# Windowed attention on one core: PV of two pairs in every second session, whole-array projections in the sessions between

## The chip, the cores and the metric

The kernel runs on one core of a Trainium2 chip. The metric is the device time of an execution in microseconds (us). The time of an execution is some 1.7 to 2.1 us longer than the span that the profile shows for it, from the first to the last instruction.

## The reference

Two problems, A and B, with inputs of the same shapes, the outputs side by side. Each of them:

```python
B, S, D = 1, 2048, 1024
H = 32; Dh = D // H; W = 256
q, k, v = split((x @ wqkv).reshape(B, S, 3, H, Dh))        # cut
scores = einsum("bhqd,bhkd->bhqk", q, k) * Dh ** -0.5
mask = (i - j >= 0) & (i - j < W)                          # causal window of 256
p = softmax(where(mask, scores, -1e9))
return einsum("bhqk,bhkd->bhqd", p, v) @ wo                # all bfloat16
```

## The kernel before

The work is cut into 152 *sessions*. In each of them TensorE computes the scores of eight half-blocks (as 32x64 tiles) into four banks of PSUM, the memory that matmuls write to; these banks exist once (`st`). ScalarE takes one exponential of all of it (128x2048 elements, 1.88 us). GpSimd masks the edges of the window. VectorE adds two masked halves (`both`). Some sessions later comes *PV*: TensorE multiplies the probabilities of a *pair* of query blocks by V, and by ones for the softmax sums, as four 32-column tiles into an accumulator `acc`, of which there are two. VectorE then takes the norm of the pair: reciprocal, two shuffles, multiply. All that is left of TensorE's time is filled with *chains*: eight steps of a projection (Q/K, V or output) into one of two PSUM buffers `pp`, which a copy then empties.

A projection step has two forms, on the whole array or as four tiles of 32 columns. A change of tiling costs some 0.1 us, in which the array empties (the *drain*), so a session with PV takes the form that PV has:

```python
def by_columns(out, lo, hi, lhsT, rhs, start, stop):
    if whole[0]:
        nc.tensor.matmul(out[:, lo:hi], lhsT=lhsT, rhs=rhs, ...)
        return
    for c in range(0, P, 32):
        nc.tensor.matmul(out[c:c + 32, lo:hi], lhsT=lhsT[:, c:c + 32], rhs=rhs, ...,
                         tile_position=(0, c))
```

The copy goes to ScalarE or VectorE, whichever a clock model, run while the program is written, expects to be done first.

The loop, which decides the order on every engine:

```python
for now in range(END):
    forced(now)                                    # chains that are needed now
    whole[0] = not (due and due[0][0] <= now)      # no PV in this session
    session(now)                                   # scores, exponential, masks
    while due and due[0][0] <= now:
        _, pg, pk = due.pop(0)
        finish_norm(1)                             # all norms but the last
        pv(pg, pk)
    while edges_due and edges_due[0][0] <= now:
        edge(*edges_due.pop(0)[1:])                # the adds of a later PV
    emit(now, level(now) - fixed[now])             # projection steps
```

## Time and profile before

| | before |
|---|---|
| time, median of 3 runs | 618.74 us (618.34 to 621.06) |
| TensorE busy | 97%, 16665 matmuls |
| 16 KB packets of the instruction queue | 132 |
| exponential on ScalarE | 152 x 1878 ns |
| copy of a projection buffer | 584 ns on ScalarE; some 0.68 us on VectorE (42 of them) |
| reciprocal on VectorE | 128 x 953 ns |

TensorE bounds the kernel, so every lost microsecond is a halt of TensorE. The view of waits lists them by line and by what released them; the columns are us in all, times, and the longest. For the kernel before, its larger lines after the start:

```profile
PE acc L562 <- issue: 4.9, 10, 1.1
PE st L490 <- issue: 2.2, 3, 1.4
...
PE pp L199 <- issue: 0.9, 2, 0.5
...
PE pp L195 <- ACT vt L207: 0.3, 1, 0.3
```

Nearly all of it is put down to "issue": no semaphore is waited for. A buffer `pp` that isn't emptied in time shows only once, for 0.3 us. The same thing from the other side, the instructions that wait for the copies on ScalarE (line 207):

```profile
who waited for it (us, times):
  ACT pt L497: 12.8, 11
  ACT osb L207: 1.6, 2
  PEld pp L855: 0.4, 1
  PE pp L195: 0.3, 1
```

### The profile page before, as it was taken

How to read it: one execution, taken by the hardware profiler on the slowest of the kernel's cores; microseconds unless marked ns; L12 is line 12 of the kernel's file. 1: busy time of each engine (PE TensorE's matmuls, PEld its weight loads, DVE VectorE, ACT ScalarE, POOL GpSimd, SP SyncE). 2: the span in 40 equal slices, each digit the busy share in tenths (PEclk: the TensorE clock that was granted, in tenths of full speed). 3: DMA queues.
4: the chain of work that ended last, by engine and by line, in shares of the span. 5: the costliest groups of instructions: out<-in, count | busy, mean ns of one | idle time of the engine just before them, and what ended most of it. 6: DMA issues, size and time to landing. Idle time of an engine off the chain costs nothing.

```text
span 616.0 us, 36878 instructions
## 1 busy us (share of the span) xinstructions
PE 598.9 (97%) x16665; PEld 372.8 (61%) x16665; DVE 429.9 (70%) x1143; ACT 405.8 (66%) x372; POOL 372.1 (60%) x918
## 2 busy tenths in 40 slices
PE   8999999999999899999999999999999999999996
PEld 4666577657665666656565766756555765555443
DVE  1388878777877678776887757777878778788200
ACT  3667766877776668666676666667766767665332
POOL 0476767776766667675766667566666766665000
PEclk9999999999999999999999999999999999999999
DMA  9814110111024410346011010112021040114221
GB/s 234 176 47 133 37 39 5 39 37 39 5 46 76 95 38 4 67 104 123 29 38 39 4 39 4 39 37 64 29 53 40 5 106 12 56 55 131 70 78 64
DMA packets 86836, 36.00 MB, mean 58 GB/s; under 512 B 65552, under 2 KB 86160, under 8 KB 86672
## 3 DMA queue, kind: packets, MB, share of 16 engines
q1 hardware_dynamic: 85632, 33.31, 22.4%
q8 instruction: 132, 2.16, 1.5%
q10 hardware_dynamic: 1040, 0.26, 0.2%
q14 instruction: 32, 0.26, 0.2%
HBM read 17.83 MB, written 8.39 MB: 43 GB/s over the span
## 4 chain that ended last, share of the span: by engine, by line
PE 90%; issue 3%; POOL 2%; DMA 2%; DVE 1%; ACT 1%; SPq 0%; POOLq 0%; ACTq 0%
PE pp L199 46%; PE pp L195 22%; PE acc L562 13%; PE st L490 9%; DMA xT<-in_A_x_dram 2%; POOL diag L507 1%; POOL pt L518 1%; DVE both L529 0%; DVE rinv L575 0%; ACT pt L497 0%; SPq L603 0%; DVE wide L580 0%; ACT osb L207 0%; DVE top L585 0%; ACT vt L207 0%
## 5 line engine op out<-in xcount | busy, mean ns | idle before, releaser
L497 ACT ACTIVATE pt<-st 128x2048 bf16<-128x2048 f32 x152 | 285.5, 1878 | 90.2 <-PE st L490 63.1
L507 POOL TENSOR_SCALAR_AFFINE_SELECT diag<-pt 128x256 bf16<-128x256 bf16 x512 | 216.3, 448 | 194.3 <-ACT pt L497 180.5
L199 PE MATMUL pp<-xT,wqk 128*32 128x512 bf16 x3092 | 185.9, 379 | 0.4 <-issue 0.4
L575 DVE RECIPROCAL rinv<-acc 128x128 f32<-128x128 f32 x128 | 121.9, 953 | 62.1 <-PE acc L562 61.4
L518 POOL TENSOR_SCALAR_AFFINE_SELECT pt<-pt 128x512 bf16<-128x512 bf16 (+1 forms) x256 | 161.0, 647 | 0.0
L529 DVE TENSOR_TENSOR both<-diag,pt 128x512 bf16<-128x512 bf16 (+1 forms) x256 | 144.8, 602 | 15.1 <-POOL diag L507 11.1
L199 PEld LDWEIGHTS <-wqk 128*32 128x32 bf16 x3092 | 83.1, 97 | 63.3 <-issue 2.0
L199 PE MATMUL pp<-wv,xT 128*32 128x256 bf16 x2840 | 88.4, 273 | 0.5 <-issue 0.5
L199 PEld LDWEIGHTS <-xT 128*32 128x32 bf16 x2840 | 75.5, 97 | 6.6 <-issue 1.1
L490 PEld LDWEIGHTS <-kT 32*64 32x64 bf16 x3904 | 41.1, 103 | 57.6 <-issue 57.4
L490 PE MATMUL st<-qT,kT 32*64 32x64 bf16 (+4 forms) x3904 | 66.3, 236 | 2.3 <-issue 2.2
L580 DVE STREAM_SHUFFLE wide<-rinv 128x128 f32<-128x128 f32 x256 | 64.5, 297 | 0.0
L207 ACT CAST osb<-pp 128x512 bf16<-128x512 f32 (+1 forms) x58 | 33.5, 578 | 46.6 <-PE pp L195 29.3
L195 PE MATMUL pp<-xT,wqk 128*128 128x512 bf16 (+1 forms) x267 | 58.8, 367 | 1.1 <-DMA xT<-in_A_x_dram 1.1
L195 PE MATMUL pp<-wo_sb,oT 128*128 128x512 bf16 (+1 forms) x269 | 58.2, 373 | 0.4 <-ACT vt L207 0.3
L199 PE MATMUL pp<-wo_sb,oT 128*32 128x512 bf16 x1004 | 58.5, 379 | 0.0
L582 DVE TENSOR_TENSOR oT<-acc,wide 128x256 bf16<-128x256 f32 x128 | 54.4, 425 | 4.4
L562 PE MATMUL acc<-pt,vt 128*32 128x128 bf16 (+2 forms) x1792 | 50.8, 224 | 1.5 <-issue 1.4
L562 PEld LDWEIGHTS <-vt 128*32 128x32 bf16 x2816 | 42.4, 96 | 15.8 <-issue 5.2
L207 ACT CAST vt<-pp 128x512 bf16<-128x512 f32 x53 | 30.9, 584 | 20.4 <-PE pp L199 14.1
L207 ACT CAST qT<-pp 128x512 bf16<-128x512 f32 x51 | 29.8, 585 | 21.5 <-PE pp L199 13.8
L195 PEld LDWEIGHTS <-oT 128*128 128x128 bf16 x269 | 25.8, 98 | 29.8 <-issue 0.8
(47 smaller groups left out, 397.3 us busy)
## 6 DMA issues: line engine op xcount, KB each, us to landing
out_dram<-osb SPq DMA_DIRECT2D x63, 128.0 KB, 1.8
wqk<-in_B_wqkv_dram SPq DMA_DIRECT2D x32, 128.0 KB, 3.0
wqk<-in_A_wqkv_dram SPq DMA_DIRECT2D x24, 128.0 KB, 3.5
wo_sb<-in_A_wo_dram SPq DMA_DIRECT2D x16, 128.0 KB, 2.9
wv<-in_B_wqkv_dram SPq DMA_DIRECT2D x16, 128.0 KB, 2.9
wo_sb<-in_B_wo_dram SPq DMA_DIRECT2D x16, 128.0 KB, 2.6
oT<-in_A_x_dram SPq DMA_DIRECT2D x4, 256.0 KB, 5.0
wv<-in_A_wqkv_dram SPq DMA_DIRECT2D x2, 512.0 KB, 4.5
```

Source lines behind the costliest of these rows:

```text
L195: nc.tensor.matmul(out[:, lo:hi], lhsT=lhsT, rhs=rhs, start=start, stop=stop, skip_group_check=True)
L199: nc.tensor.matmul(out[c:c + 32, lo:hi], lhsT=lhsT[:, c:c + 32], rhs=rhs, start=start, stop=stop, tile_position=(0, c), skip_group_check=True)
L207: nc.scalar.copy(out=out, in_=in_)
L490: nc.tensor.matmul(scores[c * HALF:(c + 1) * HALF, r, a * HALF:(a + w_) * HALF], lhsT=kT[rows, keys], rhs=qT[rows, q:q + w_ * HALF], start ...
L497: nc.scalar.activation(out=pt[:, :, :n * HALF], in_=scores[:, :, :n * HALF], func=ACT.Exp, bias=-SHIFT, scale=cfg.scale)
L507: nc.gpsimd.affine_select(out=diags[(g, p)][:, :, h, lo:lo + HALF], in_=pt[:, :, a * HALF:(a + 1) * HALF], pattern=[[0, 4], [1, HALF]], co ...
L518: nc.gpsimd.affine_select(out=blk, in_=blk, pattern=[[0, 4], [-1, w_ * HALF]], compare_op=ALU.is_gt, fill=0.0, base=-HALF * (us[a][2] - 3) ...
L529: nc.vector.tensor_tensor(out=both[:, :, h, o:o + w_], in0=dg[:, :, h, o:o + w_], in1=pts[t][:, :, a:a + w_], op=ALU.add)
L562: nc.tensor.matmul(acc[32 * r:32 * r + 32, o:o + w_], lhsT=lhsT, rhs=src[:, r, :], start=(x == 0), stop=(x == len(moves) - 1), tile_positi ...
L575: nc.vector.reciprocal(out=inverses[0][:, turn % 2, :], in_=acc[:, 2 * P:3 * P])
L580: nc.vector.stream_shuffle(out=wide[:, h * P:(h + 1) * P], in_=inverses[0][:, turn % 2, :], mask=[16 * h] * 32)
L582: nc.vector.tensor_tensor(out=oTs[(pi, k)][:, t, (p % 2) * 256:(p % 2 + 1) * 256], in0=acc[:, 0:256], in1=wide[:], op=ALU.mult)
```

## The change

The intent: PV of two pairs is gathered in every second session (`PV_EVERY`), so that the sessions between have no PV and can run their projections on the whole array. That saves six of eight instructions a step. One more buffer each for the probabilities and the diagonal, and one x tile less to pay for them. The norms are finished ahead of a session with PV, and the adds stand ahead of it too.

```diff
-PT_BUFS = 5
-DG_BUFS = 4
+PT_BUFS = 6
+DG_BUFS = 5
+X_AHEAD = 1
+PV_EVERY = 2
@@
-    xpool = ctx.enter_context(tc.tile_pool(name="xT", bufs=NQ + 2))
+    xpool = ctx.enter_context(tc.tile_pool(name="xT", bufs=NQ + X_AHEAD))
@@
+    def edge_time(g, p):
+        return max(when(g, *e) for e in entries if e[1] // 2 == p) + PV_LAG - 1
+
     def pv_time(g, p):
-        return max(when(g, *e) for e in entries if e[1] // 2 == p) + PV_LAG
+        return -(-(edge_time(g, p) + 1) // PV_EVERY) * PV_EVERY
@@ def x_time(pi, k):
-        if k < 2:
+        if k < X_AHEAD:
             return begin(pi * T - 3) + 2 * k
-        return first_use(pi * T - 1, k - 2, 0) + 1
+        return first_use(pi * T - 1, k - X_AHEAD, 0)
@@
-    edges_due = [(d - 1, g, p) for d, g, p in due if p]
+    edges_due = [(edge_time(g, p), g, p) for _, g, p in due if p]
@@ in the loop, after the PV of this session
             finish_norm(1)
             pv(pg, pk)
+        if due and due[0][0] == now + 1:
+            finish_norm()
         while edges_due and edges_due[0][0] <= now:
             edge(*edges_due.pop(0)[1:])
```

## The prediction

> **What bounds the kernel now.** I read the page first: busy shares, granted clock, the chain that ended last.
>
> ```profile
> PE 598.9 (97%) x16665; PEld 372.8 (61%) x16665; DVE 429.9 (70%) x1143; ACT 405.8 (66%) x372; POOL 372.1 (60%) x918
> PEclk9999999999999999999999999999999999999999
> q8 instruction: 132, 2.16, 1.5%
> PE 90%; issue 3%; POOL 2%; DMA 2%; DVE 1%; ACT 1%; SPq 0%; POOLq 0%; ACTq 0%
> ```
>
> TensorE is busy 97% at full clock and carries 90% of the chain, so only its own stream and its pauses can move the end. Then the timeline of TensorE over two neighbouring sessions, the first without PV (projections on the whole array, 128*128), the second with PV (projections as four 32-column tiles, 128*32):
>
> ```profile
> 407.81 0.42 PE L490 MATMUL st<-qT,kT 32*64 32x192 bf16 x20
> 408.17 3.41 PE L195 MATMUL pp<-xT,wqk 128*128 128x512 bf16 x15
> 411.51 0.43 PE L490 MATMUL st<-qT,kT 32*64 32x64 bf16 x28
> 411.87 0.41 PE L562 MATMUL acc<-pt,vt 128*32 128x128 bf16 x12
> ...
> 412.44 1.47 PE L199 MATMUL pp<-xT,wqk 128*32 128x512 bf16 x24
> 413.73 1.48 PE L199 MATMUL pp<-wv,xT 128*32 128x256 bf16 x48
> ```
>
> The reader is to take start-to-start distances, because the durations overlap. 24 column matmuls are 6 groups of four: 413.73 - 412.44 = 1.29 us, 215 ns a group. 15 whole matmuls and the drain before the next scores: 411.51 - 408.17 = 3.34 us, or 15 x 216 ns and 0.1. So a 512-wide projection step costs 216 ns in both forms, and I find 109 against 109 ns for the 256-wide ones by the same reading. Each kind of session has about 0.50 us that is not streaming of PV or projections: 3.70 - 15 x 0.2133 for the first, 3.63 - 0.53 - 6 x 0.2133 - 12 x 0.1067 for the second.
>
> Last, what stops the stream: the timeline where a session takes 4.68 us rather than 3.6, and the DMA view of its start (211.9 to 213.1).
>
> ```profile
> 212.41 0.47 PE L490 MATMUL st<-qT,kT 32*64 32x64 bf16 x36
> 212.81 0.41 PE L562 MATMUL acc<-pt,vt 128*32 128x64 bf16 x20
> 213.05 0.28 PE L562 MATMUL acc<-diag,vt 128*32 128x128 bf16 x6
> 214.41 0.23 PE L562 MATMUL acc<-diag,vt 128*32 128x128 bf16 x2 [1.08 <-issue]
> ```
>
> ```profile
> q8 instruction: 1, 0.02, 5.0%
> ```
>
> TensorE halts after six of eight equal matmuls, in the middle of a group of four, where no semaphore is waited for. The idle time is put down to issue. In that stretch one packet of queue 8, the instruction queue, starts (at 212.03 by the trace's DMA records). I put the whole trace against the program order. Sixteen gaps between starts exceed 0.4 us in the same way. Their first matmul stands each time at place 194 or 195 modulo 256 of TensorE's program, and each comes 2.17 to 3.15 us after a packet of queue 8 began. Together they cost 11.2 us. Two packets of queue 8 never start less than 3.23 us apart. So these are waits for the next block of 256 instructions, and they come where instructions are short: scores, PV and 32-column V projections.
>
> **What the Trainium skill says.** "Runtime: NRT & Kernel Launch", section "Instruction fetch mechanics": the sequencer refills its memory in 16 KiB blocks of 256 instructions over its own DMA queue. The trace agrees: 132 packets, 2.16 MB, 16 KB each, and a halt only at block boundaries. The page also calls the cost of a crossing "mostly hidden"; 11.2 us are not hidden here. "TensorEngine Tiling (Array Packing)", section "Key Properties": a change of tiling mode drains the array. The trace agrees, with 96 to 107 ns beyond the stream ahead of each scores block. Its section "Restrictions" says that column tiling disables fast weight load, which would make whole-array projections cheaper. The trace shows no gain: loads of 97 to 98 ns in both forms, and 216 ns a step in both.
>
> **The change, part by part.**
>
> 1. *Whole-array projections in every second session.* From the program listings of the two kernels: groups of four column matmuls go from 1734 (773 Q/K, 710 V, 251 output) to 992 (402, 437, 153); whole ones go from 802 to 1544. Matmul work is the same. 742 steps convert at 0 ns each by the distances above, so the stream gains nothing. Each saves three loads and three matmuls: 742 x 6 = 4452 instructions of 33,330, 13%, or 17 of 130 blocks.
>
> 2. *PV of two pairs in one session.* The same 128 pairs, the same matmuls. Sessions with PV go from 119 of 152 to 75. A session has two mode changes either way (scores to PV and columns, or scores to whole, and back), and 0.50 us fixed in both kinds. Adding the read distances over both instruction lists, from the first scores to the last projection, gives 576.8 us before and 576.2 after: **-0.6 us**.
>
> 3. *The block waits.* Fewer instructions, but bunched: a double session has 256 to 368 (for instance 32 scores, 84 PV and 60 column matmuls, two instructions each, 352), one without PV 66 to 114 (before: 176 to 360 with PV, most of them under 280). I take for each block boundary the summed distances of the 288 instructions ahead of it (a block and the 32 by which I take the sequencer to lead) and compare this with a refill of 3.6 us, an estimate from packets of 3.2 to 4.4 us apart around the halts. Before: 20 of 128 blocks are shorter, by 5.4 us. After: 15 of 111, by 7.5 us; the worst takes only 2.1 us, the worst before 2.9. At 3.8 us it is 10.6 against 10.9. If a late refill also delays the next, it is 9.1 against 7.5 us at 3.6, and 17.5 against 10.9 at 3.8. This places most of the sixteen halts correctly, which is why I trust its form, though single halts come out too small. Fewer crossings in danger, each worse. I choose **-2.5 us** of the 11.2.
>
> 4. *Norms and adds ahead.* VectorE per pair: 0.953 for the reciprocal, 2 x 0.252 of shuffle, 0.425 for the multiply, half of 0.52, and 1.13 of adds: 3.27 us. Before, no TensorE halt of over 0.4 us falls on an accumulator or an add, so there is no wait to remove. After, two pairs bring 6.5 us of VectorE work into two sessions. In the first half these last 2 x 3.2 us by my sum, in the second 2 x 3.6. In the listing both norms stand ahead of the adds for the next pairs, so a late norm delays the adds, which end the next PV. At most three double sessions follow each other before a single one, so the debt stays below a microsecond: **+1.3 us**, perhaps 0.3 us in one of three double sessions of the first half.
>
> 5. *One x tile less, PT and diagonal buffers one more each.* Loads of the second problem's x come later and closer, 24 pieces of 3.6 us from issue to landing, and one session near the boundary grows to 6.6 us by my count while its neighbours shrink. The work is moved, not added: 0.
>
> Sum: -0.6 - 2.5 + 1.3 = -1.8 us. 618.7 - 1.8 = **617 us**.
>
> **The rivals.**
>
> *Fetch waits vanish.* If thinner sessions let the fetch run far enough ahead, all 11.2 us go: 618.7 - 0.6 - 11.2 = 607 us. For it: 13% fewer instructions, and a sparse session ahead of every dense one. Against it: the halts show one block of lead at most, and a double session can pass a whole block in 2.1 us.
>
> *Fetch waits get worse.* If most of the 48 sessions with 72 or more PV matmuls paid 0.3 us more than I take, it would be some 10 us: about 627 us. For it: blocks as short as 2.1 us, never seen before. Against it: the position of the boundaries varies, so most double sessions start with a fetched block in hand.
>
> *VectorE takes over.* With 6.5 us and a copy of 0.67 us in a 6.4 us double session, TensorE would wait for `both` or for an accumulator. Half a microsecond in each of some 25 double sessions of the first half would be +12 us, some 9 if the single ones between pay part of it back: about 625 us. Against it: VectorE is at 70%, and the listing gives it fewer copies than before.
>
> *Whole-array weight loads are faster after all.* At 5 ns a step, 742 steps would be 3.7 us: 613 us. The distances speak against it.
>
> **Range and chances.** The rivals reach 607 and 627, and neither is likely in full. The range is **610 to 623.5 us**. Faster by over 2% is below 606.4, which needs every fetch wait gone and no new wait: **4%**. Slower by over 2% is above 631, which needs a new regular wait: **5%**. Within 2%: **91%**.
>
> **What would show each step right or wrong.** Step 1: about 402 + 437 + 153 groups on the column line, at 216 and 109 ns from start to start. Step 2: the same fixed 0.50 us in both kinds of session. Step 3: 113 to 116 packets on queue 8, halts put down to issue and still ending 2.2 to 3.2 us after one, at fewer places, now in or just after the PV of double sessions. Step 4: TensorE waits of 0.2 to 0.6 us ahead of the last PV matmuls, ended by the adds, before 300 us and not after. Step 5: no TensorE wait on x between 190 and 300 us. I am wrong if the fetch waits fall below 4 us or rise above 15, if VectorE waits pass 5 us, or if a session without PV turns out to be bound by the exponential instead.

## More of the kernel before

The instructions of an engine stand in its program in the order in which they were emitted:

```python
def evacuate(out, in_, engines=("act", "dve")):
    if clock.evacuate(engines) == "act":
        nc.scalar.copy(out=out, in_=in_)
    else:
        nc.vector.tensor_copy(out=out, in_=in_)
```

## The result, and the profile after

| | before | after |
|---|---|---|
| time, median | 618.81 us (4 runs) | 623.56 us (623.12 to 624.22, 4 runs) |
| ratio | | 1.007 [1.0044, 1.0097] |
| span of the profiled execution | 616.0 us | 622.5 us |

Within 2%, but slower, where 1.8 us faster was predicted. The median lies at the upper edge of the predicted range, 0.06 us beyond it. Both kernels were run once more beside each other later: 615.78 us for before, 623.23 us for after, ratio 1.0125 [1.0102, 1.0147]. The loss is real.

The page of the changed kernel: busy times and counts, the instruction queue, and the chain that ended last.

```profile
PE 591.0 (95%) x14363; PEld 362.2 (58%) x14439; DVE 394.8 (63%) x1126; ACT 411.1 (66%) x389; POOL 360.6 (58%) x918
...
q8 instruction: 115, 1.88, 1.3%
...
PE 31%; POOL 4%; issue 3%; ACT 2%; DVE 0%; POOLq 0%; ACTq 0%
```

Three readings. There are 76 fewer matmuls than weight loads: records missing from this trace (the repeat has all 14439), so "PE 95%" is a little low and some lines of issue below are only holes in the record. ScalarE has 17 instructions more than before, VectorE 17 fewer: copies of projection buffers have moved from VectorE to ScalarE. And the shares of the chain add up to only some 40%, because it could not be followed back further; it isn't used.

The view of waits of TensorE in the changed kernel, same columns as above:

```profile
PE pp L197 <- issue: 7.7, 47, 0.4
PE pp L201 <- issue: 3.3, 6, 0.9
PE pp L197 <- ACT vt L209: 2.7, 6, 0.6
PE pp L197 <- ACT qT L209: 2.2, 5, 0.5
PE pp L197 <- ACT kT L209: 1.7, 5, 0.5
...
PE pp L197 <- ACT osb L209: 0.7, 2, 0.5
PE pp L197 <- POOL xT L382: 0.6, 1, 0.6
PE acc L567 <- DVE both L534: 0.3, 1, 0.3
```

The first line is mostly missing records (it is absent in the repeat). What is new are the four lines "<- ACT ... L209": a whole-array projection waits until a copy on ScalarE has emptied its buffer. From the side of the copies, in the same trace:

```profile
who waited for it (us, times):
  ACT pt L502: 29.3, 26
  PE pp L197: 7.4, 18
  ACT osb L209: 4.5, 6
```

TensorE waits for them 18 times where it was once, and always on the line of whole-array projections.

The views name only part of each halt, so I summed them from the trace itself: distances from the start of one matmul to the start of the next beyond what the first one streams, those over 0.12 us, after the first 16.2 us. A halt is called *block* where it comes at the place, modulo 256 instructions of TensorE's program, at which the prediction found its sixteen, and 2.1 to 3.6 us after a packet of the instruction queue began; the others are sorted by the two matmuls they lie between. Halts between two projection matmuls are called *buffer* (a copy is what releases nearly all of those for which the view names a releaser; one of 0.73 us in the changed kernel waits for an x tile instead), halts inside PV *PV* (an accumulator or the adds). The traces of before and both repeats are complete; sums from traces that lack records are less sure.

| us of halts (number) | block | buffer | PV | other | packets | span |
|---|---|---|---|---|---|---|
| before | 11.96 (24) | 1.05 (4) | 0.12 (1) | 0 | 132 | 616.0 |
| after | 6.57 (12) | 14.00 (31) | 0.48 (1) | 0.18 | 115 | 622.5 |
| before, repeated | 12.49 (23) | 1.02 (3) | 0.37 (1) | 0 | 132 | 616.2 |
| after, repeated | 5.19 (10) | 14.63 (32) | 0.48 (1) | 0.18 | 115 | 621.4 |

The spans differ by 6.5 us: -5.4 of block waits, +12.95 of buffers, +0.4 in PV, +0.2 elsewhere, which leaves -1.6 for everything else. In the repeat the same sum is -7.3 + 13.6 + 0.1 + 0.2, and -1.4 is left of the 5.2 us. So the change did take away about half of the block waits, and paid about twice as much (12.95 for 5.4 us, 13.6 for 7.3) with a wait that the kernel before hardly had.

What such a wait looks like: the timeline of a session without PV in the changed kernel (start, duration, engine, line, operation, count, and in brackets the idle time before it with what ended it).

```profile
123.18 0.42 PE L495 MATMUL st<-qT,kT 32*64 32x256 bf16 x20
...
123.73 1.88 ACT L502 ACTIVATE pt<-st 128x2048 bf16<-128x2048 f32 x1 [1.48 <-PE st L495]
123.76 1.89 PE L197 MATMUL pp<-xT,wqk 128*128 128x512 bf16 x8 [0.16 <-issue]
...
124.27 0.94 DVE L580 RECIPROCAL rinv<-acc 128x128 f32<-128x128 f32 x1
...
125.50 0.58 ACT L209 CAST qT<-pp 128x512 bf16<-128x512 f32 x1
125.79 0.42 DVE L587 TENSOR_TENSOR oT<-acc,wide 128x256 bf16<-128x256 f32 x1
125.97 0.60 ACT L209 CAST kT<-pp 128x512 bf16<-128x512 f32 x1
...
126.13 1.02 PE L197 MATMUL pp<-xT,wqk 128*128 128x512 bf16 x4 [0.48 <-ACT qT L209]
```

The same place in the repeat, whose trace lacks no matmul:

```profile
123.29 2.12 PE L197 MATMUL pp<-xT,wqk 128*128 128x512 bf16 x9
125.89 1.02 PE L197 MATMUL pp<-xT,wqk 128*128 128x512 bf16 x4 [0.48 <-ACT qT L209]
```

Before the scores, TensorE had all but the last step of a Q chain. The first step after the scores (the record that is missing in the first trace; the repeat has nine matmuls in place of eight) ends it, and from then on its buffer can be emptied. But ScalarE has just begun the exponential of 1.88 us, and VectorE is taking the norms of two pairs until after 126. So the copy waits until 125.5. TensorE meanwhile has eight steps for the other buffer, 8 x 0.216 = 1.73 us, fewer than exponential and copy together (1.88 + 0.58 = 2.46 us), and stands until the copy is done. In a session with PV, the PV matmuls lie between the scores and the projections, and take up much of that difference (0.57 us for one pair, from 411.87 to 412.44 in the timeline of the prediction).

### The profile page after: what moved, and what is told of

It reads as the page before. It is cut to its first block, busy times and chain, and to the rows that moved or that the text cites. A ratio compares the mean times of both kernels' runs of the same rounds, so it can differ in the third digit from the quotient of the medians. Undisturbed runs are those within 1.5% of the kernel's fastest.

```text
span 622.5 us, 32360 instructions
## 1 busy us (share of the span) xinstructions
PE 591.0 (95%) x14363; PEld 362.2 (58%) x14439; DVE 394.8 (63%) x1126; ACT 411.1 (66%) x389; POOL 360.6 (58%) x918
## 3 DMA queue, kind: packets, MB, share of 16 engines
q8 instruction: 115, 1.88, 1.3%
## 5 line engine op out<-in xcount | busy, mean ns | idle before, releaser
L534 DVE TENSOR_TENSOR both<-diag,pt 128x512 bf16<-128x512 bf16 (+1 forms) x256 | 117.4, 499 | 69.4 <-PE acc L567 52.2
L197 PE MATMUL pp<-xT,wqk 128*128 128x512 bf16 (+1 forms) x580 | 138.6, 373 | 13.4 <-issue 5.6
L197 PEld LDWEIGHTS <-wqk 128*128 128x128 bf16 x638 | 58.9, 98 | 72.6 <-issue 11.0
L201 PE MATMUL pp<-xT,wqk 128*32 128x512 bf16 x1608 | 97.4, 379 | 0.3 <-issue 0.2
L197 PE MATMUL pp<-wo_sb,oT 128*128 128x512 bf16 (+1 forms) x349 | 78.1, 374 | 3.2 <-issue 1.6
L197 PE MATMUL pp<-wv,xT 128*128 128x256 bf16 x587 | 71.6, 273 | 3.1 <-ACT kT L209 1.5
L209 ACT CAST osb<-pp 128x512 bf16<-128x512 f32 (+1 forms) x63 | 36.4, 579 | 43.3 <-PE pp L197 28.4
L197 PEld LDWEIGHTS <-xT 128*128 128x128 bf16 x587 | 55.5, 98 | 15.8 <-issue 4.6
L201 PEld LDWEIGHTS <-wqk 128*32 128x32 bf16 x1608 | 41.8, 97 | 32.5 <-issue 1.2
L201 PE MATMUL pp<-wv,xT 128*32 128x256 bf16 x1748 | 55.6, 273 | 3.1 <-issue 3.1
L201 PEld LDWEIGHTS <-xT 128*32 128x32 bf16 x1748 | 46.0, 97 | 8.6 <-issue 4.7
```

The lines of the kernel that those rows point to most:

```text
L197: nc.tensor.matmul(out[:, lo:hi], lhsT=lhsT, rhs=rhs, start=start, stop=stop, skip_group_check=True)
L534: nc.vector.tensor_tensor(out=both[:, :, h, o:o + w_], in0=dg[:, :, h, o:o + w_], in1=pts[t][:, :, a:a + w_], op=ALU.add)
```

## The experiments

The theory (T): the loss is the copy of a projection buffer that stands in ScalarE's order behind the exponential, in a session without PV, while VectorE, which could take it, is held by the norms that were put ahead. Rivals: (R1) VectorE's bunched norms and adds alone, which would show as waits in PV; (R2) instruction blocks, now needed faster in the double sessions; (R3) the whole-array form itself; (R4) the one x tile less. There were twelve runs, in three groups, the last group for repeats; each group has its own runs of the kernel before on its own chip (medians 618.84, 615.88 and 615.78 us), so I compare by ratio. All results were correct.

### The changed kernel without the norms put ahead

```diff
-        if due and due[0][0] == now + 1:
-            finish_norm()
```

> The changed kernel without the call that puts all norms ahead of the adds and copies in the session before a PV session; everything else kept. Theory (TensorE now waits for projection buffers in sessions without PV, because the exponential holds ScalarE and the bunched norms hold VectorE): VectorE gets free for copies earlier, so the buffer waits fall from about 12.8 us to 5 to 9 us and the time is 616 to 621 us. Rival (late adds and norms hold up PV, so putting them ahead helps): waits of PV for accumulators appear and the time is 626 us or more. If neither placement matters: 622 to 625 us.

Measured: 619.13 us, ratio 1.0006 [0.9976, 1.0035]. Buffer halts 4.94 us (from 14.00), block halts 4.97, but PV halts 8.26 us in 12 places (from 0.48). With VectorE no longer busy at this place, it takes 34 of the copies from ScalarE (355 instructions there, from 389), and most of the buffer waits go. What comes instead was no part of the theory, which therefore got its time (616 to 621 us) with one wait traded for another; the rival had named waits for accumulators. The timeline between the two PVs of a double session in this kernel:

```profile
122.25 0.28 PE L567 MATMUL acc<-both,ones 128*32 128x128 bf16 x8
...
123.06 0.42 DVE L587 TENSOR_TENSOR oT<-acc,wide 128x256 bf16<-128x256 f32 x1
...
123.53 0.41 PE L567 MATMUL acc<-pt,vt 128*32 128x64 bf16 x20 [1.00 <-DVE oT L587]
```

and its line in the view of waits:

```profile
PE acc L567 <- DVE oT L587: 6.1, 9, 1.1
```

The second PV needs the accumulator of the pair before, whose norm is only now being taken. So the two added lines do a job: two pairs in one session use up both accumulators, and both norms must be done before. They are needed, and they cost some 9 us of buffer waits where they stand.

### The changed kernel with PV in every session again

```diff
-PV_EVERY = 2
+PV_EVERY = 1
```

> The changed kernel with PV in every session again (pairs not bunched), with the one x tile less, the extra buffers and the norms put ahead kept. Theory: PV lies between the scores and the projections again, so the first projection chain ends after the exponential does and buffer waits fall under 4 us; halts for instruction blocks return to about 12 us; time 617 to 622 us. If the x tile or the norms' place cause the loss, the time stays at 623 to 626 us.

Measured: 628.73 us, ratio 1.0173 [1.0138, 1.0207]: a miss, slower than the changed kernel, whose ratio was 1.007 and 1.0125. Buffer halts fell to 2.14 us, as T has it (sessions without PV become few), and block halts are 7.97 us with 132 packets. But PV halts are 10.53 us in 29 places. In the view of waits, and in the timeline of one session:

```profile
PE acc L567 <- DVE both L534: 5.3, 15, 0.5
```

```profile
100.85 1.39 DVE L534 TENSOR_TENSOR both<-diag,pt 128x512 bf16<-128x512 bf16 x2
...
101.52 0.24 PE L567 MATMUL acc<-both,ones 128*32 128x128 bf16 x4
102.29 0.24 PE L567 MATMUL acc<-both,ones 128*32 128x128 bf16 x4 [0.53 <-DVE both L534]
```

PV now comes in nearly every session, so "the next session has PV" holds nearly always, the norm of the pair just accumulated is finished at once, and the adds stand behind it. That is R1, in the place in which the prediction had looked for it, but it takes this kernel to show it: the changed kernel has one such halt. The lines that put norms ahead belong to a plan with gaps between PVs.

### The changed kernel with projections in columns everywhere

```diff
-        whole[0] = not (due and due[0][0] <= now)
+        whole[0] = now < 4
```

> The changed kernel with all projections of the main loop as four 32-column matmuls. Theory (the whole-array form only saves instructions, hence instruction blocks): the buffer waits in sessions without PV stay at 10 to 13 us, the packets on queue 8 rise from 115 to about 148, the halts at block boundaries rise from 7 to 12 to 25 us; time 628 to 640 us. Rival (the whole-array form is faster by the step or by its drains): the same rise without more halts. If instruction blocks don't matter: 622 to 625 us.

Measured: 645.06 us, ratio 1.042 [1.0386, 1.0455], more than expected. Its instruction queue and its waits:

```profile
q8 instruction: 145, 2.38, 1.6%
```

```profile
PE pp L201 <- issue: 9.0, 13, 1.4
PE st L495 <- issue: 6.7, 12, 1.1
...
PE pp L201 <- ACT vt L209: 2.9, 7, 0.6
PE pp L201 <- ACT qT L209: 2.5, 6, 0.5
```

Buffer halts are 12.4 us (28), as in the changed kernel: they do not depend on the form of the projection, so R3 falls as their cause. Block halts are 25.25 us in 37 places, with 145 packets. That is R2 working the other way: more instructions for the same multiplications make more of these waits. Of the 21.8 us between the two spans (644.3 and 622.5 us), block halts make 18.7 and buffer halts -1.6; the other 4.7 us are not accounted for, so it is not shown that the column form costs nothing else.

### The changed kernel with an open chain finished ahead of the scores

In a session without PV, the chain that has begun is completed before the scores, so its copy is emitted before the exponential:

```diff
         forced(now)
+        if current and not (due and due[0][0] <= now):
+            emit(now, sum(ns for ns, _ in current))
         whole[0] = not (due and due[0][0] <= now)
         session(now)
```

> The changed kernel, but ahead of the scores of a session without PV the projection chain already begun is finished, so that its copy stands on ScalarE ahead of the exponential. Theory: one of the two buffers is free when the exponential starts, the buffer waits fall from about 12.8 us to under 4 us, and the time is 611 to 616 us, below both kernels. Rival (the waits come from elsewhere, or the later exponential holds up the next scores): 622 us or more.

Measured: 614.99 us, ratio 0.9939 [0.9908, 0.997]. Buffer halts 0.14 us, from 14.00, and the norms still stand ahead: T, by the direct edit. The copies are divided as in the changed kernel (386 instructions on ScalarE and 1129 on VectorE, where that has 389 and 1126), so it is their place that counts. The edit has one side effect: the steps moved ahead keep the form of the session before, often columns, so there are 420 matmuls more and 118 packets. The timeline of the same stretch of the program in this kernel:

```profile
126.31 0.42 PE L495 MATMUL st<-qT,kT 32*64 32x256 bf16 x20
126.43 0.58 ACT L209 CAST qT<-pp 128x512 bf16<-128x512 f32 x1 [1.14 <-PE pp L201]
126.66 2.76 PE L197 MATMUL pp<-xT,wqk 128*128 128x512 bf16 x11
...
126.91 1.88 ACT L502 ACTIVATE pt<-st 128x2048 bf16<-128x2048 f32 x1
```

The copy runs while TensorE does the scores, and the exponential follows it. TensorE goes on without a break. The price is a later exponential, which now sometimes holds the scores of the next session (PSUM banks `st`):

```profile
PE st L495 <- ACT pt L502: 2.6, 5, 0.8
```

That and PV halts of 1.23 us are far less than what was saved.

### Norms put off to the end of the session, in both versions

```diff
-        if due and due[0][0] == now + 1:
-            finish_norm()
         while edges_due and edges_due[0][0] <= now:
             edge(*edges_due.pop(0)[1:])
         emit(now, level(now) - fixed[now])
+        if due and due[0][0] == now + 1:
+            finish_norm()
```

On the changed kernel:

> The changed kernel with the bunched norms issued at the end of the session before a PV session, after its projections and their copies, in place of at its start. Theory (norms ahead of the copies hold the projection buffers; norms that are not done hold the second pair's accumulator): buffer waits near the 4.7 us of the kernel without the call, waits of the second pair for its accumulator well under the 8.3 us there, 1 to 4 us; time 613 to 618 us. If only the missing of PV ahead of the projections matters, buffer waits stay at 10 us or more and the time at 621 to 624 us.

and on the version with the chain finished first:

> Both mends together: the begun chain is finished ahead of the scores of a session without PV, and the norms are issued at the end of that session. Theory: buffer waits stay at about 0, the accumulator waits are 1 to 4 us, so no better than finishing the chain alone: 614 to 618 us. If the two add up: 610 to 613 us.

Measured: 620.23 us, ratio 1.0067 [1.005, 1.0084], and 621.67 us, ratio 1.01 [1.0068, 1.0131]. Both times are misses. The first has buffer halts of 4.74 us, as expected, but PV halts of 8.11 us, the same as with the two lines removed; the second has PV halts of 6.86 us and 1.81 us more between scores and PV. I had thought that the norms only had to be done at some time before the next PV. At the end of the session is too late: the accumulator is still held when the second PV begins. In the view of waits, first the one, then the other:

```profile
PE acc L567 <- DVE oT L587: 6.1, 9, 1.1
```

```profile
PE acc L567 <- DVE oT L587: 7.4, 10, 1.3
```

So the norms have to stand early, and the copy has to be kept out of their way. This is what the chain finished first does.

### The kernel before with whole-array projections in every session

```diff
-        whole[0] = not (due and due[0][0] <= now)
+        whole[0] = True
```

> The kernel before with all projections on the whole array, also right after a PV in the same session. Theory: a session with PV then has one more mode change, 0.10 to 0.13 us each in 119 sessions, 12 to 15 us in all, and the packets on queue 8 fall from 132 to about 92, with the halts at block boundaries falling from 12.0 us to under 3 us; time 617 to 626 us. If the halts are not due to blocks of instructions, they stay at 10 to 12 us and the time is 630 us or more. If whole-array steps are faster in themselves, it is under 614 us.

Measured: 615.46 us, ratio 0.9992 [0.9975, 1.0009], a little faster than expected. Its instruction queue:

```profile
q8 instruction: 92, 1.51, 1.0%
```

That is 92 packets, and **no** block halt at all, from 11.96 us. So R2's waits go entirely when the instructions become few enough. It gains nothing, because each session with PV now has one change of tiling more. The two neighbouring lines of its timeline:

```profile
411.08 0.28 PE L562 MATMUL acc<-both,ones 128*32 128x128 bf16 x8
411.29 0.94 PE L195 MATMUL pp<-wv,xT 128*128 128x256 bf16 x7
```

The median distance from the start of the last PV matmul to the first whole-array one is 151 ns, where the kernel before has 45 ns to the first column matmul: 106 ns more. (This trace lacks 123 matmuls, and both ends are recorded in 48 sessions only; a complete trace of the last version below has 152 ns.) The drain before the next scores, counted from the start of the last step's first matmul, is 96 ns in place of 107. That is 95 ns in each of some 118 sessions, 11.2 us, against 12 us of block waits saved.

### The kernel before with one x tile less

`X_AHEAD = 1` with its buffer count and its load times, and nothing else of the change.

> The kernel before with one x tile less alone, its loads placed as in the changed kernel. Theory: the tile has no part in the result, 617 to 621 us with about 12 us of block halts. Rival (later, closer loads of x hold up work near the change of problem): 622 us or more, with new waits between 190 and 310 us.

Measured: 618.98 us (617.05 to 619.98), ratio 1.0056 [1.0036, 1.0076]. Its trace, which is that of its fastest run, has no wait of TensorE for an x tile and no more halts than the kernel before (block 10.08, buffer 1.18, PV 0.48 us). In the changed kernel one halt of 0.73 us at 248.9 us is released by the memset that prepares an x tile. The ratio says that the tile costs about 3 us here, and no trace shows where; the kernel before of this group was not traced. Beside a loss of 4.8 to 7.5 us for the whole change (by the medians) that isn't small, so R4 stays open. It isn't needed for the sums above, in which one halt of 0.73 us is all that waits for an x tile, and the version with the chain finished first has the loss gone with one tile less.

### The repeats

The two kernels and the best version once more, in five rounds each, and the best version with whole-array projections in every session:

> The kernel before, unchanged, as a run of its own with a profile, beside the changed ones on one chip: ratio 1.000 within 0.003. It shows how far block halts differ by chip and run: theory, between 8 and 14 us, and the time follows them.

> The changed kernel, unchanged, again: ratio 1.005 to 1.012; buffer waits in sessions without PV of 12 to 15 us, block halts of 4 to 8 us. If the sum of the two does not repeat, the account of the first trace was chance.

> The changed kernel with the begun chain finished ahead of the scores of a session without PV, again: ratio 0.990 to 0.998 to before, buffer waits about 0, block halts 4 to 9 us.

> The same with whole-array projections also after PV. Theory: about 75 more mode changes of 0.09 to 0.11 us, 7 to 8 us, against block halts of about 7 us that go to 0; ratio 0.990 to 0.999 to before. If block halts can be had back without cost (mode changes hidden): 0.985 or less. If the instruction blocks no longer matter: 1.003 or more.

The last column is the view's line `PE st <- ACT pt`, the others are sums as above:

| | median (runs) | ratio to before | block | buffer | PV | scores behind an exponential |
|---|---|---|---|---|---|---|
| before, as another kernel | 616.62 (6) | 1.0007 [0.9985, 1.0029] | 12.49 | 1.02 | 0.37 | 0 |
| after | 623.23 (6) | 1.0125 [1.0102, 1.0147] | 5.19 | 14.63 | 0.48 | 0 |
| after, chain finished first | 614.59 (6) | 0.9986 [0.9961, 1.0011] | 6.13 | 0.36 | 1.38 | 2.6 |
| the same, whole array everywhere | 614.58 (6) | 0.9983 [0.9964, 1.0002] | 0 | 0 | 1.71 | 2.2 |

The runs of before against itself (1.0007) show how much a ratio of this group can be trusted. The repair of the changed kernel holds: 8.6 us better than the changed kernel by the medians, and its buffer halts are gone again. Its ratio to before, 0.9986, is just outside the expected 0.990 to 0.998, and the changed kernel's 1.0125 just outside 1.005 to 1.012; the other two came as expected. The last row also has one halt of 0.72 us in none of the columns, for a load of weights. Against the kernel before, it is ahead by 0.6% in one group and not certainly ahead in the other. None of these versions clearly beats the kernel before by more than about half a per cent. Whole-array projections everywhere take away its last block waits and give them back as drains, as in the kernel before.

One more thing can be seen in the times. The kernel before scatters from 614.05 to 619.95 us over 11 runs of this group. The two kernels without block waits scatter by 0.44 us (the last row of the table, 6 runs) and by 0.47 us (whole-array projections in the kernel before, 4 runs, in a group in which the kernel before scatters by 1.6 us over 7). It looks as if the block waits are most of the jitter from run to run; no trace of several executions of one kernel was compared halt by halt.

## Why the prediction was right or wrong

"Within 2%" was right, with 91%. The centre, 617 us, was 6.6 us too low, and the sign of the change was wrong. By its own steps:

1. *Whole-array projections convert at 0 ns.* Right. The line of column matmuls has 1608 + 1748 + 612 records, which are the 402 + 437 + 153 groups of four of the listing, and the stream gained nothing by it. "TensorEngine Tiling (Array Packing)", "Restrictions", let one hope for more; the measured step decided.

2. *The stream, -0.6 us.* Consistent: what the measured halts leave of the difference is -1.6 us, in the repeat -1.4. (One of the readings is a little off: the sum given for a session with PV comes to 0.54 us, not 0.50.)

3. *The block waits, -2.5 us.* Right in sign and mechanism (115 packets, halts at block ends, 145 packets making 25.25 us and 92 making none), wrong in size: -5.4 us in the first pair of traces, -7.3 in the second. The sign was partly a choice: the two plain counts in the prediction went up (5.4 to 7.5 and 10.6 to 10.9 us), and only those with a delayed refill went down. The lead of 32 instructions in them was assumed, and no run measures it. Perhaps the counts gave the sparse sessions between too little credit; that isn't shown. Nor are the halts inside PV any more: in the repeat they lie in the column projections after it and in the scores. The first rival ("Fetch waits vanish") went in the right direction, and the second, that they get worse, fell.

4. *Norms and adds ahead, +1.3 us.* This is the step that failed. It asked only whether PV waits for the adds, and that came out at +0.4 us, from one halt of 0.48 us. It never asked what else stands in line behind two norms. The copies do. With the norms bunched into the session without PV, VectorE is taken, the copy goes to ScalarE behind the exponential, and TensorE waits for the projection buffer: +12.95 us. Taking the norms away from there cut these waits from 14.00 to 4.94 us; putting the copy ahead of the exponential cut them to 0.14 us. In the third rival, "VectorE takes over", I even wrote against it that "the listing gives it fewer copies than before". That was a sign and not a comfort: 17 copies had moved to ScalarE. Their number alone isn't the cause, since the version with the chain finished first divides the copies nearly the same way; their place behind the exponential is. The time of that rival, about 625 us, is near what came, but its reason, waits for `both` or an accumulator, is not what the trace shows.

5. *One x tile less, 0.* Not quite: one halt of 0.73 us at 248.9 us in the changed kernel (counted among the buffer halts above), where the prediction said that none would come; what it costs alone (ratio 1.0056) is open.

Put together: predicted -0.6 - 2.5 + 1.3 + 0 for the buffers = -1.8 us; measured -1.6 - 5.4 + 0.4 + 12.95 + 0.2 = +6.5 us between the profiled spans. The last clause of the prediction, "if a session without PV turns out to be bound by the exponential instead", named the place, but nothing in the sum was worked out for it, though the numbers for it were all at hand: 1.88 + 0.58 us on ScalarE against 8 x 0.216 us on TensorE. "Trainium Kernel Development and Optimization", section "Best Practices", has a warning near to this that I passed over, "Mind PSUM pressure: TensorE tiling speeds up compute but not PSUM evacuation". The evacuation did become the limit, with 18 waits of TensorE for copies on ScalarE where there was one; but it is not tiling that made it so, since the buffer halts are 14.00 us with whole-array projections and 12.4 us with tiled ones.

Two errors of opposite sign, a gain twice as large as thought and a wait not thought of, left a total that was only 1% off. That was luck. Had only the total been looked at, the estimate would have seemed nearly right.

## What to carry to other kernels

When work is gathered to spare mode changes or instructions, follow the small copies that free PSUM buffers: where they stand in the order of each engine, what long operation may come ahead of them, and how many steps the other buffer gives TensorE in the meantime. A copy emitted just ahead of a long operation instead of just behind it was worth 8.6 us here. And count instructions as well as streamed columns: many short tiled matmuls can run dry the fetch of the instructions themselves, where the same multiplications in fewer instructions do not.

## What the Trainium skill lacked or had wrong

- "Runtime: NRT & Kernel Launch", section "Instruction fetch mechanics", calls the cost of a block crossing "mostly hidden". On TensorE it was 12.0 us of 616 with 132 blocks, 25.3 us with 145 and 0 with 92. The block size that it gives, 16 KiB, agrees (132 packets, 2.16 MB).
- The same section gives TensorE room for 2048 instructions, eight blocks, and in a note below speaks of only two lines of 16 KiB. The runs show no sign of a lead of eight blocks: in the kernel before, halts of up to 1.5 us come at the same place modulo 256 and end 2.2 to 3.2 us after a packet began, and these packets never begin less than 3.23 us apart. The lead itself was not measured.
- "TensorEngine Tiling (Array Packing)", section "Key Properties", has the drain at a change of tiling without its size: here 106 ns more from PV to a whole-array matmul than from PV to a column one (151 against 45 ns), and some 0.10 us ahead of the scores.
- The same page, section "Restrictions", says that column tiling disables fast weight load, but not whether a step gets longer by it. Here it doesn't: loads of 97 to 98 ns and 216 ns a step in both forms.
- No page that I read says that column tiling is paid for in instructions: eight a step in place of two, and with them the block waits of the first point.
